# Attention into a GELU feed-forward on one core: V's path, the transposes' layout and the order of the start are changed

## The chip, the cores and the metric

One core of one Trainium2 chip runs the whole program. The metric is device time in microseconds; lower is better. Three runs of the kernel before took 374.42, 374.43 and 375.52 us, so its median is 374.43 us.

## What is computed

Attention is done inside chunks of 64 tokens, for 8 batches, 8 heads, 576 tokens (9 chunks) and head size 64. The heads' outputs stand side by side as 512 features of 4608 tokens, and these go through a feed-forward layer with exact GELU:

```python
q_c = q.reshape(B, H, nc, chunk, D)          # chunk = 64, D = 64
scores = scale * np.matmul(q_c, k_c.transpose(0, 1, 2, 4, 3))
attn = softmax(scores)
out = np.matmul(attn, v_c)
x = out.transpose(0, 2, 1, 3).reshape(B * S, H * D)   # 4608 x 512
h = x @ w_in                                           # 512 x 2048
y = gelu(h) @ w_out                                    # 2048 x 512
```

All inputs and the output are f32; the kernel computes its products in bf16.

## The kernel before, in words

The 4608 tokens are cut into 9 tiles of 512 tokens (8 chunks). A tile's attention has 4 groups `g`, each of 2 heads, and each group has three steps.

- **T** (`att_T`): TensorE transposes 4 pieces of Q and 4 of K into one PSUM tile `tp` (two such tiles exist). VectorE copies Q's half to `qT` and K's half, in two copies, into the block-diagonal `k_bd` (six exist; the off-diagonal blocks are zeroed once).
- **S** (`att_S`): 8 small matmuls give the scores `s_ps`, ScalarE applies Exp into `pT`.
- **B** (`att_B`): one matmul sums `pT`, 8 small ones multiply it with the block-diagonal `v_bd` into `av_ps`. VectorE transposes the sums (`t`), takes reciprocals (`r`), spreads them (`rc`) and multiplies (`x`).

`s_ps`, `sum_ps` and `av_ps` take turns in three PSUM buffers, so a B waits until an earlier user of its buffer is done.

The feed-forward of a tile has two phases of 16 slots: `mm1_slot` does 4 matmuls of 512 columns and a GELU on ScalarE, `mm2_slot` does 4 matmuls, and after each fourth slot VectorE copies `y_ps` to `y_sb` and SP stores it. The order of all engines is written out by hand: while tile t is in mm1 and tile t-1 in mm2, the steps T, S and B of tile t+1 are put between slots (`run_phase`, lines 232 to 267). Exp and GELU need different ScalarE tables, so each change from one to the other costs a table load.

Three queues bring data. SP issues the Q and K loads (line 98), f32, in pieces of 1 KB, and the stores. POOL issues the V loads (line 124) and the weight loads (lines 243 and 247), which change f32 to bf16 on the way; V's pieces are rows of 64 f32. POOL also casts Q and K of all tiles but the first (line 115). Its instructions run in order:

```python
new_tile(0)        # q, k on SP; 8 V loads on POOL; casts on VectorE and ScalarE
...                # 4 loads of w_in on POOL
new_tile(1)        # 16 V loads on POOL
...                # 2 loads of w_out on POOL
new_tile(2)        # 16 V loads on POOL
T, S_, Bs = att_units(0)
...
T, S_, Bs = att_units(1)     # tile 1's casts on POOL, behind all of these
```

A tile's 16 token columns of one transposed piece stand four tokens apart, and the kernel before carries this order through: `qT` keeps it, the copies into `k_bd` (line 157) and the multiplication into `x` (line 190) put it right as they write, so they write 2-byte elements 8 bytes apart.

Of the kernel before, what the change touches and what calls it, by code (L numbers as in the profile page):

```python
# [11 lines left out]
def kernel(  # L12
# [21 lines left out]
    CT = MT // CH  # L34
    G = H // 2
# [5 lines left out]
    FF = d_ff // P  # L41
# [15 lines left out]
    for i, t_ in enumerate(v_bds):
        nc.vector.memset(t_[0:CH, :, :, CH:P], 0.0)
        nc.vector.memset(t_[CH:P, :, :, 0:CH], 0.0)
    for t_ in k_bds:  # L60
        nc.vector.memset(t_[0:CH, :, CH:P], 0.0)
        nc.vector.memset(t_[CH:P, :, 0:CH], 0.0)
# [6 lines left out]
    ld = ctx.enter_context(tc.tile_pool(name="ld", bufs=3))  # L69
    work = ctx.enter_context(tc.tile_pool(name="work", bufs=3))  # L70
# [7 lines left out]
    def segments(t):  # L78

        segs = []  # L80
        c = t * CT
        while c < (t + 1) * CT:
            b, cs = divmod(c, NC)
            n = min(NC - cs, (t + 1) * CT - c)
            segs.append((c - t * CT, b, cs, n))
            c += n
        return segs

    def load_qk(t):
        st = {}  # L90
        raw = {nm: ld.tile([P, H, J, D], f32, tag=nm + "f", name=f"{nm}_f32", bufs=2) for nm in "qk"}
        for nm in "qk":
            st[nm] = ld.tile([P, G, J, 2, D], bf16, tag=nm, name=f"{nm}_nat", bufs=2)
        parts = [(h0, h0 + 2) for h0 in range(0, H, 2)] if t == 0 else [(0, H)]
        for h0, h1 in parts:
            for nm, src in (("q", q), ("k", k)):
                for i0, b, cs, n in segments(t):
                    nc.sync.dma_start(
                        raw[nm][PC * i0:PC * (i0 + n), h0:h1],
                        src[b, h0:h1, CH * cs:CH * (cs + n), :].rearrange(  # L100
                            "h (p j) d -> p h j d", j=J),
                    )
        def cast():
            for h0, h1 in parts:
                for nm in "qk":
                    o = st[nm][:, h0 // 2:h1 // 2].rearrange("p g j r d -> p g r j d")
                    i_ = raw[nm][:, h0:h1].rearrange("p (g r) j d -> p g r j d", r=2)
                    for g in range((h1 - h0) // 2):
                        if t == 0:
                            if nm == "q":  # L110
                                nc.vector.tensor_copy(o[:, g], i_[:, g])
                            else:
                                nc.scalar.copy(o[:, g], i_[:, g])
                        else:
                            nc.gpsimd.tensor_copy(o[:, g], i_[:, g])  # L115
        st["cast"] = cast
        return st

    def load_v(t):
        v_bd = v_bds[t % NV]  # L120
        for g in range(G):
            for r in range(2):
                for i0, b, cs, n in segments(t):
                    nc.gpsimd.dma_start(  # L124
                        v_bd[CH * r:CH * (r + 1), i0:i0 + n, g, CH * r:CH * (r + 1)],
                        v[b, 2 * g + r, CH * cs:CH * (cs + n), :].rearrange(
                            "(i key) d -> key i d", key=CH),
                    )
        return v_bd

    tiles = {}

    def new_tile(t):
        st = load_qk(t)
        st["v"] = load_v(t)
        tiles[t] = st
        if t == 0:
            st["cast"]()
# [34 lines left out]
    def att_B(t, g):  # L173
        st = tiles[t]
        pT = st["pT", g]
        sum_ps = ps_at.tile([P, CT * CH], f32, tag="at", name="sum_ps")
        nc.tensor.matmul(sum_ps[:], ones_bd[:], pT[:], start=True, stop=True)  # L177
        av_ps = ps_at.tile([P, CT, CH], f32, tag="at", name="av_ps")
        for i in range(CT):
            nc.tensor.matmul(av_ps[:, i, :], st["v"][:, i, g, :], pT[:, i, :],  # L180
                             start=True, stop=True)
        NB = MT // 32
        t1 = work.tile([P, NB, 32], f32, tag="t1", name="t1")
        nc.vector.transpose(t1[:], sum_ps[:].rearrange("p (n e) -> p n e", e=32))  # L184
# [47 lines left out]
    def run_phase(slot_fn, t, n, extra):  # L232
        for s in range(n):
            for u in extra.get(s, ()):
                u()
            slot_fn(t, s)

    with tc.manual_schedule():
        new_tile(0)
# [4 lines left out]
        new_tile(1)  # L244
# [53 lines left out]
```

## Time and profile before

| | |
|---|---|
| median of the runs | 374.43 us |
| the profiled execution, its own time | 375.98 us |
| its span, from first to last instruction | 374.2 us |
| TensorE busy | 305.2 us, 82% of the span |
| VectorE busy | 239.6 us, 64% |
| ScalarE busy | 140.2 us, 37% |
| POOL busy | 125.2 us, 33% (without its DMA issues' waits) |
| HBM read / written | 36.70 / 9.44 MB |

The shares are means over stages that differ: a start, a long stretch in which the tiles repeat, and an end. The stages are read apart below. All positions are microseconds from the start of the span.

### The profile page before, as it was taken

The page shows a single profiled execution, that of the slowest core. Times are in us where ns is not written, and L with a number is a line of the kernel's source. Part 1 is how long each engine was busy: PE and PEld are TensorE (multiplying, and loading weights), DVE is VectorE, ACT ScalarE, POOL GpSimd, SP SyncE. Part 2 cuts the span into 40 slices and gives each one's busy share as a digit, 9 for nine tenths or more (in the row PEclk, how much of TensorE's full clock was granted, in tenths as well). Part 3 has the DMA queues.
Part 4 walks back from the last instruction along what each step waited for, and adds up shares of the span by engine and source line. Part 5 has one row for each costly group of instructions (what it writes and reads, how often), then busy time and mean ns, then how long its engine had stood idle before and what let it go on. Part 6 is the DMA issues. An engine that isn't in the chain of part 4 may idle for free.

```text
span 374.2 us, 5238 instructions
## 1 busy us (share of the span) xinstructions
PE 305.2 (82%) x2052; PEld 154.5 (41%) x2052; DVE 239.6 (64%) x313; ACT 140.2 (37%) x208; POOL 125.2 (33%) x204
## 2 busy tenths in 40 slices
PE   0353500766899999999999999999999999999995
PEld 0241100332454555455445544544544455444442
DVE  7989100696775975887598589759867965920221
ACT  2130200189564066236505622551563165254000
POOL 7321855989700007703920780270130000000000
PEclk9999955598999999999999999999999999999999
DMA  9999899894700094848649483890800200010212
GB/s 209 256 247 243 56 174 98 145 127 29 46 2 29 30 228 66 102 119 161 66 50 218 71 85 108 198 84 30 257 26 28 87 0 30 30 56 0 86 56 84
DMA packets 67352, 37.57 MB, mean 100 GB/s; under 512 B 40192, under 2 KB 62720, under 8 KB 67328
## 3 DMA queue, kind: packets, MB, share of 16 engines
q1 hardware_dynamic: 24224, 28.32, 28.4%
q0 software_dynamic: 43104, 8.92, 26.9%
q8 instruction: 16, 0.26, 0.3%
q14 instruction: 8, 0.07, 0.1%
HBM read 36.70 MB, written 9.44 MB: 123 GB/s over the span
## 4 chain that ended last, share of the span: by engine, by line
PE 65%; DVE 14%; DMA 13%; POOL 4%; issue 2%; DVEq 0%; POOLq 0%
PE h_ps L212 30%; PE y_ps L224 28%; DMA w_in_sb<-in_moe_w_in_dram 7%; DVE x L190 4%; DMA w_out_sb<-in_moe_w_out_dram 4%; PE tp L148 4%; POOL v_bd L124 3%; DMA v_bd<-in_v_dram 3%; DVE rc L188 3%; DVE k_bd L157 3%; DVE t L184 3%; PE s_ps L167 1%; PE av_ps L180 1%; PE sum_ps L177 1%; DVE r L186 1%
## 5 line engine op out<-in xcount | busy, mean ns | idle before, releaser
L212 PE MATMUL h_ps<-x,w_in_sb 128*128 128x512 bf16 x576 | 138.1, 390 | 4.4 <-DVE x L190 4.3
L214 ACT ACTIVATE h<-h_ps 128x512 bf16<-128x512 f32 x144 | 85.5, 597 | 144.7 <-PE h_ps L212 144.5
L224 PE MATMUL y_ps<-w_out_sb,h 128*128 128x512 bf16 x576 | 132.5, 379 | 0.0
L124 POOL DMA_DIRECT2D v_bd<-in_v_dram x128 | 83.9, 713 | 29.4 <-DMA w_in_sb<-in_moe_w_in_dram 12.8
L157 DVE COPY k_bd<-tp 64x512 bf16<-64x512 bf16 x72 | 92.6, 1287 | 0.5
L212 PEld LDWEIGHTS <-w_in_sb 128*128 128x128 bf16 x576 | 55.7, 100 | 65.4 <-issue 9.3
L224 PEld LDWEIGHTS <-h 128*128 128x128 bf16 x576 | 53.5, 98 | 58.1
L228 DVE COPY y_sb<-y_ps 128x512 f32<-128x512 f32 x36 | 24.5, 695 | 60.4 <-PE y_ps L224 60.4
L115 POOL CAST q_nat<-q_f 128x512 bf16<-128x512 f32 x32 | 18.4, 637 | 106.8 <-PE h_ps L212 58.6
L190 DVE TENSOR_TENSOR x<-av_ps,rc 128x512 bf16<-128x512 f32 x36 | 46.5, 1292 | 4.1 <-DVE rc L188 0.5
L150 DVE COPY qT<-tp 128x512 bf16<-128x512 bf16 x36 | 15.2, 423 | 51.6 <-PE tp L148 51.4
L148 PE MATMUL tp<-ident,q_nat 128*128 128x128 bf16 x144 | 15.5, 236 | 39.7 <-POOL q_nat L115 22.6
L170 ACT ACTIVATE pT<-s_ps 128x512 bf16<-128x512 f32 x36 | 21.4, 597 | 34.9 <-PE s_ps L167 34.0
L148 PEld LDWEIGHTS <-q_nat 128*128 128x128 bf16 x144 | 11.7, 106 | 50.3 <-POOL q_nat L115 23.1
L184 DVE STREAM_TRANSPOSE t<-sum_ps 128x512 f32<-128x512 f32 x36 | 25.7, 715 | 8.8 <-PE sum_ps L177 8.8
L188 DVE STREAM_TRANSPOSE rc<-r 128x512 f32<-128x512 f32 x36 | 25.6, 711 | 1.3
L180 PEld LDWEIGHTS <-v_bd 128*128 128x128 bf16 x288 | 14.1, 101 | 23.4 <-issue 17.5
L180 PE MATMUL av_ps<-pT,v_bd 128*128 128x64 bf16 x288 | 15.4, 198 | 9.8 <-DVE x L190 5.8
L115 POOL CAST k_nat<-k_f 128x512 bf16<-128x512 f32 x32 | 18.4, 628 | 8.5 <-DMA k_f<-in_k_dram 7.8
L214 ACT ACT_TABLE_LOAD x12 | 15.4, 1283 | 10.6 <-PE h_ps L212 10.4
L167 PEld LDWEIGHTS <-k_bd 128*128 128x128 bf16 x288 | 13.9, 102 | 12.5 <-DVE k_bd L157 3.7
L177 PE MATMUL sum_ps<-pT,ones_bd 128*128 128x512 bf16 x36 | 14.8, 411 | 4.9 <-DVE x L190 4.8
(24 smaller groups left out, 88.5 us busy)
## 6 DMA issues: line engine op xcount, KB each, us to landing
out_dram<-y_sb SPq DMA_DIRECT2D x36, 256.0 KB, 2.0
w_in_sb<-in_moe_w_in_dram POOLq DMA_DIRECT2D x4, 512.0 KB, 23.0
w_out_sb<-in_moe_w_out_dram POOLq DMA_DIRECT2D x2, 1024.0 KB, 11.3
q_f<-in_q_dram SPq DMA_DIRECT2D x2, 896.0 KB, 9.1
k_f<-in_k_dram SPq DMA_DIRECT2D x2, 896.0 KB, 11.5
q_f<-in_q_dram SPq DMA_DIRECT2D x6, 256.0 KB, 6.8
k_f<-in_k_dram SPq DMA_DIRECT2D x6, 256.0 KB, 7.4
q_f<-in_q_dram SPq DMA_DIRECT2D x2, 768.0 KB, 11.6
```

The lines of the kernel that those rows point to most:

```text
L115: nc.gpsimd.tensor_copy(o[:, g], i_[:, g])
L124: nc.gpsimd.dma_start(v_bd[CH * r:CH * (r + 1), i0:i0 + n, g, CH * r:CH * (r + 1)], v[b, 2 * g + r, CH * cs:CH * (cs + n), :].rearrange("( ...
L148: nc.tensor.transpose(tp[:, w, j, :], st[nm][:, g, j].rearrange("p r d -> p (r d)"), ident[:])
L157: nc.vector.tensor_copy(k_bd[sl, :, sl].rearrange("p i (c j) -> p j i c", j=J), tp[sl, 1].rearrange("p j (i c) -> p j i c", i=CT))
L180: nc.tensor.matmul(av_ps[:, i, :], st["v"][:, i, g, :], pT[:, i, :], start=True, stop=True)
L184: nc.vector.transpose(t1[:], sum_ps[:].rearrange("p (n e) -> p n e", e=32))
L188: nc.vector.transpose(rc[:], r1[:].to_broadcast([P, NB, 32]))
L190: nc.vector.tensor_tensor(x[:, g, :].rearrange("p (i c j) -> p i j c", i=CT, j=J), av_ps[:].rearrange("p i (j c) -> p i j c", j=J), rc[:]. ...
L212: nc.tensor.matmul(h_ps[:], w_in_sb[:, ks, f * P:(f + 1) * P], st["x"][:, ks, :], start=(ks == 0), stop=(ks == KS - 1))
L214: nc.scalar.activation(st["h"][:, f, :], h_ps[:], Act.Gelu)
L224: nc.tensor.matmul(y_ps[:], st["h"][:, f, ms * P:(ms + 1) * P], w_out_sb[:, f, :], start=(f == 0), stop=(f == FF - 1))
L228: nc.vector.tensor_copy(y_sb[:], y_ps[:])
```

## The change

V is loaded by SP as f32 rows into a buffer `vf`, and cast from there into `v_bd`: tile 0's by ScalarE and POOL in two halves each, the other tiles' by POOL in two casts. The f32 buffers of Q and K are single now. The copies after the transposes and the multiplication into `x` all write in natural order; the copies read PSUM with the stride instead. Tile 0's casts go to VectorE, ScalarE and POOL, and one of its two `k_bd` copies to ScalarE. The zeroing of `v_bd` 1 and 2 and of `k_bd` 4 and 5 goes to POOL. In mm1 of tile 0, the steps of tile 1 stand in slots 10 to 15 and behind it (they stood in slots 4 to 15).

```diff
-        raw = {nm: ld.tile([P, H, J, D], f32, tag=nm + "f", name=f"{nm}_f32", bufs=2) for nm in "qk"}
+        raw = {nm: ld.tile([P, H, J, D], f32, tag=nm + "f", name=f"{nm}_f32", bufs=1) for nm in "qk"}
+        vf = ld.tile([P, G, CT, D], f32, tag="vf", name="v_f32", bufs=1)
...
-                    nc.gpsimd.dma_start(
-                        v_bd[CH * r:CH * (r + 1), i0:i0 + n, g, CH * r:CH * (r + 1)],
+                    nc.sync.dma_start(
+                        vf[CH * r:CH * (r + 1), g, i0:i0 + n, :],
                         v[b, 2 * g + r, CH * cs:CH * (cs + n), :].rearrange(
                             "(i key) d -> key i d", key=CH),
...
+        def cast_v(r, copy, gs=slice(0, G)):
+            sl = slice(CH * r, CH * (r + 1))
+            copy(v_bd[sl, :, gs, sl].rearrange("p i g d -> p g i d"), vf[sl, gs])
...
-        qT = work.tile([P, CT, J, PC], bf16, tag="qT", name="qT", bufs=6)
+        qT = work.tile([P, CT, CH], bf16, tag="qT", name="qT", bufs=6)
         nc.vector.tensor_copy(
-            qT[:].rearrange("p i j c -> p j i c"),
-            tp[:, 0].rearrange("p j (i c) -> p j i c", i=CT))
+            qT[:].rearrange("p i (c j) -> p i c j", j=J),
+            tp[:, 0].rearrange("p j (i c) -> p i c j", i=CT))
...
-            nc.vector.tensor_copy(
-                k_bd[sl, :, sl].rearrange("p i (c j) -> p j i c", j=J),
-                tp[sl, 1].rearrange("p j (i c) -> p j i c", i=CT))
+            copy = nc.scalar.copy if t == 0 and r == 1 else nc.vector.tensor_copy
+            copy(k_bd[sl, :, sl].rearrange("p i (c j) -> p i c j", j=J),
+                 tp[sl, 1].rearrange("p j (i c) -> p i c j", i=CT))
...
         nc.vector.tensor_tensor(
-            x[:, g, :].rearrange("p (i c j) -> p i j c", i=CT, j=J),
-            av_ps[:].rearrange("p i (j c) -> p i j c", j=J),
-            rc[:].rearrange("p n e -> p (n e)").rearrange("p (i j c) -> p i j c", i=CT, j=J),
-            op=mybir.AluOpType.mult)
+            st["x"][:, g, :], av_ps[:].rearrange("p i e -> p (i e)"),
+            rc[:].rearrange("p n e -> p (n e)"), op=mybir.AluOpType.mult)
...
+    def pool_casts(t):
+        for g in range(G):
+            for nm in "qk":
+                tiles[t]["cast"](nm, g, nc.gpsimd.tensor_copy)
+        for r in range(2):
+            tiles[t]["cast_v"](r, nc.gpsimd.tensor_copy)
...
-        run_phase(mm1_slot, 0, FF, {4: [T[0]], 5: [T[1]], 6: [T[2]], 7: [T[3]],
-                                    9: [S_[0]], 10: [S_[1]], 11: [S_[2], Bs[0]], 12: [S_[3]],
-                                    13: [Bs[1]], 14: [Bs[2]], 15: [Bs[3]]})
+        run_phase(mm1_slot, 0, FF, {10: [T[0]], 11: [T[1]], 12: [T[2], S_[0]], 13: [T[3], S_[1]],
+                                    14: [S_[2]], 15: [S_[3], Bs[0]]})
+        for u in Bs[1:]:
+            u()
```

POOL's queue at the start, before. `v_bd_67`, `_68` and `_69` belong to tiles 0, 1 and 2; `q_f_154` and `k_f_155` are tile 1's Q and K.

```order
L124 DMA v_bd_67<-in_v_dram 64x8x64 x7
L243 DMA w_in_sb<-in_moe_w_in_dram 128x4x512 x4
L124 DMA v_bd_68<-in_v_dram 64x64
...
L247 DMA w_out_sb<-in_moe_w_out_dram 128x8x512 x2
L124 DMA v_bd_69<-in_v_dram 64x2x64
...
L115 CAST q_nat<-q_f_154 128x2x4x64 x4
L115 CAST k_nat<-k_f_155 128x2x4x64 x4
```

And of the change, the same place (`q_f_254` and `k_f_255` are tile 1's):

```order
L120 CAST q_nat<-q_f_106 128x2x4x64 x2
L251 DMA w_in_sb<-in_moe_w_in_dram 128x4x512 x4
L124 CAST v_bd_67<-v_f_108 64x2x8x64 x2
...
L60 MEMSET v_bd_68 64x32x64
L61 MEMSET v_bd_68 64x32x64
L120 CAST q_nat<-q_f_254 128x2x4x64
L120 CAST k_nat<-k_f_255 128x2x4x64
...
L124 CAST v_bd_68<-v_f_256 64x4x8x64 x2
L270 DMA w_out_sb<-in_moe_w_out_dram 128x8x512 x2
```

Tile 1's casts stood behind 40 loads of V and all the weights; now they stand behind the 4 loads of w_in, tile 0's casts of V and some zeroing, and the loads of w_out stand behind them.

SP's queue at the start, of the change, with what each DMA waits for (`DMAHW0` to `DMAHW7` are the counters of DMAs on this queue; a later DMA on a counter waits for the landing of the one before it, here eight DMAs earlier).

```order
L105 DMA k_f_107<-in_k_dram 128x2x256
L113 DMA v_f_108<-in_v_dram 64x8x64 [waits DMAHW0_49]
L113 DMA v_f_108<-in_v_dram 64x8x64 [waits DMAHW1_49]
...
L105 DMA q_f_254<-in_q_dram 16x8x256 [waits DMAHW0_49,DVE_49,Pool_49]
L105 DMA q_f_254<-in_q_dram 112x8x256 [waits DMAHW1_49]
L105 DMA k_f_255<-in_k_dram 16x8x256 [waits DMAHW2_49,Activation_49]
L105 DMA k_f_255<-in_k_dram 112x8x256 [waits DMAHW3_49]
L113 DMA v_f_256<-in_v_dram 64x64 [waits DMAHW5_49,DMAHW6_49,DMAHW4_49,DMAHW7_49,Activation_49,Pool_49]
```

Tile 1's Q and K came directly behind tile 0's on this queue; now tile 0's V stands between them, they wait for tile 0's casts, and tile 1's V waits for tile 0's casts of V.

## Rows read from the trace of the kernel before

**Rows 1.** Busy time by stage: us, each engine's busy time (count), PEclk, DMA share, GB/s.

```profile
43.70:66.30 22.60, 0.03 (x1) 0.00 (x0) 0.00 (x0) 0.60 (x1) 14.20 (x23) 0.56 1.03 121
66.30:96.70 30.40, 21.18 (x151) 10.71 (x152) 23.33 (x28) 19.60 (x24) 29.40 (x50) 0.82 0.80 97
96.70:329.40 232.70, 226.84 (x1597) 116.10 (x1597) 176.78 (x224) 101.34 (x155) 63.31 (x103) 1.00 0.45 86
```

**Rows 2.** Waits, first 100 us: who waited for whom, total us, times, longest.

```profile
PE tp L148 <- POOL q_nat L115: 22.6, 1, 22.6
POOL v_bd L124 <- DMA w_in_sb<-in_moe_w_in_dram: 12.8, 4, 3.7
```

**Rows 3.** POOL in order of time: start, us, instruction, [idle before, releaser].

```profile
59.87 5.76 POOL L124 DMA_DIRECT2D v_bd<-in_v_dram  x9 [4.82 <-DMA w_out_sb<-in_moe_w_out_dram]
65.52 2.39 POOL L115 CAST q_nat<-q_f 128x512 bf16<-128x512 f32 x4
```

**Rows 4.** The chain that ended last: start, us, what.

```profile
95.38 1.29 DVE x L190
...
129.40 0.86 PE h_ps L212 x4
...
162.56 0.86 PE h_ps L212 x4
```

**Rows 5.** PE in steady state, in order of time.

```profile
120.30 0.44 PE L180 MATMUL av_ps<-pT,v_bd 128*128 128x64 bf16 x8 [0.83 <-DVE x L190]
```

**Rows 6.** DMA queues of the whole span: packets, MB, share of 16 engines.

```profile
q1 hardware_dynamic: 24224, 28.32, 28.4%
q0 software_dynamic: 43104, 8.92, 26.9%
```

**Rows 7.** Busy time by stage, as Rows 1, of two stretches full of loads.

```profile
48.00:58.00 10.00, 0.00 (x0) 0.00 (x0) 0.00 (x0) 0.00 (x0) 3.47 (x6) 0.50 1.19 190
...
2.30:38.90 36.60, 11.62 (x104) 7.80 (x105) 32.23 (x49) 6.03 (x9) 12.44 (x19) 1.00 1.27 247
```

**Rows 8.** DMA issues: count, KB each, us from issue to landing.

```profile
out_dram<-y_sb SPq DMA_DIRECT2D x36, 256.0 KB, 2.0
```

**Rows 9.** Groups by line and form: count, busy us, mean ns, idle before and releasers.

```profile
L157 DVE COPY k_bd<-tp 64x512 bf16<-64x512 bf16 x72 | 92.6, 1287 | 0.5
L190 DVE TENSOR_TENSOR x<-av_ps,rc 128x512 bf16<-128x512 f32 x36 | 46.5, 1292 | 4.1 <-DVE rc L188 0.5
L228 DVE COPY y_sb<-y_ps 128x512 f32<-128x512 f32 x36 | 24.5, 695 | 60.4 <-PE y_ps L224 60.4
L115 POOL CAST q_nat<-q_f 128x512 bf16<-128x512 f32 x32 | 18.4, 637 | 106.8 <-PE h_ps L212 58.6 <-DMA q_f<-in_q_dram 48.2
L150 DVE COPY qT<-tp 128x512 bf16<-128x512 bf16 x36 | 15.2, 423 | 51.6 <-PE tp L148 51.4
```

**Rows 10.** VectorE in order of time: the starts of two B groups.

```profile
90.57 0.72 DVE L184 STREAM_TRANSPOSE t<-sum_ps 128x512 f32<-128x512 f32 x1 [0.49 <-PE sum_ps L177]
...
93.52 0.72 DVE L184 STREAM_TRANSPOSE t<-sum_ps 128x512 f32<-128x512 f32 x1
```

**Rows 11.** ScalarE in order of time.

```profile
41.12 0.60 ACT L214 ACTIVATE h<-h_ps 128x512 bf16<-128x512 f32 x1 [1.11 <-PE h_ps L212]
42.82 0.60 ACT L214 ACTIVATE h<-h_ps 128x512 bf16<-128x512 f32 x1 [1.11 <-PE h_ps L212]
...
79.41 0.60 ACT L170 ACTIVATE pT<-s_ps 128x512 bf16<-128x512 f32 x1
80.02 1.28 ACT L214 ACT_TABLE_LOAD   x1
...
83.22 0.60 ACT L170 ACTIVATE pT<-s_ps 128x512 bf16<-128x512 f32 x1
...
98.44 0.60 ACT L214 ACTIVATE h<-h_ps 128x512 bf16<-128x512 f32 x1 [0.71 <-PE h_ps L212]
99.30 0.60 ACT L214 ACTIVATE h<-h_ps 128x512 bf16<-128x512 f32 x1 [0.27 <-PE h_ps L212]
```

More of the change, by code (lines that the diff above doesn't have):

```diff
@@ L56, with zero_v, zero_k @@
     k_bds = [consts.tile([P, CT, P], bf16, name=f"k_bd{i}") for i in range(NK)]
[L57 to L62, printed above, removed]
+    def zero_v(i):
+        eng = nc.vector if i == 0 else nc.gpsimd
+        eng.memset(v_bds[i][0:CH, :, :, CH:P], 0.0)
+        eng.memset(v_bds[i][CH:P, :, :, 0:CH], 0.0)
+    def zero_k(k_bd, eng):
+        eng.memset(k_bd[0:CH, :, CH:P], 0.0)
+        eng.memset(k_bd[CH:P, :, 0:CH], 0.0)
     w_in_sb = consts.tile([P, KS, d_ff], bf16, name="w_in_sb")
@@ L87, in segments, with load @@
         return segs
-    def load_qk(t):
+    def load(t):
         st = {}
-        raw = {nm: ld.tile([P, H, J, D], f32, tag=nm + "f", name=f"{nm}_f32", bufs=2) for nm in "qk"}
+        raw = {nm: ld.tile([P, H, J, D], f32, tag=nm + "f", name=f"{nm}_f32", bufs=1) for nm in "qk"}
+        vf = ld.tile([P, G, CT, D], f32, tag="vf", name="v_f32", bufs=1)
         for nm in "qk":
             st[nm] = ld.tile([P, G, J, 2, D], bf16, tag=nm, name=f"{nm}_nat", bufs=2)
+        v_bd = v_bds[t % NV]
+        st["v"] = v_bd
         parts = [(h0, h0 + 2) for h0 in range(0, H, 2)] if t == 0 else [(0, H)]
@@ L102, in load_qk @@
                     )
[L103 to L120, printed above, removed]
         for g in range(G):
@@ L128, in load_v, with cast @@
                     )
-        return v_bd
-    tiles = {}
[L133 to L138, printed above, removed]
+        def cast(nm, g, copy):
+            copy(st[nm][:, g].rearrange("p j r d -> p r j d"), raw[nm][:, 2 * g:2 * g + 2])
+        def cast_v(r, copy, gs=slice(0, G)):
+            sl = slice(CH * r, CH * (r + 1))
+            copy(v_bd[sl, :, gs, sl].rearrange("p i g d -> p g i d"), vf[sl, gs])
+        st["cast"], st["cast_v"] = cast, cast_v
+        tiles[t] = st
+    tiles = {}
     kcount = [0]
@@ L188, in att_B @@
         nc.vector.transpose(rc[:], r1[:].to_broadcast([P, NB, 32]))
-        x = st["x"]
         nc.vector.tensor_tensor(
-            x[:, g, :].rearrange("p (i c j) -> p i j c", i=CT, j=J),
-            av_ps[:].rearrange("p i (j c) -> p i j c", j=J),
-            rc[:].rearrange("p n e -> p (n e)").rearrange("p (i j c) -> p i j c", i=CT, j=J),
-            op=mybir.AluOpType.mult)
+            st["x"][:, g, :], av_ps[:].rearrange("p i e -> p (i e)"),
+            rc[:].rearrange("p n e -> p (n e)"), op=mybir.AluOpType.mult)
     def att_units(t):
-        if t:
-            tiles[t]["cast"]()
         tiles[t]["x"] = xpool.tile([P, G, MT], bf16, tag="x", name="x")
@@ L236, in run_phase @@
             slot_fn(t, s)
-    with tc.manual_schedule():
-        new_tile(0)
+    def pool_casts(t):
[4 more added lines that the diff above has]
+            tiles[t]["cast_v"](r, nc.gpsimd.tensor_copy)
+    with tc.manual_schedule():
+        zero_v(0)
+        load(0)
+        T, S_, Bs = att_units(0)
+        c0 = tiles[0]["cast"]
+        c0("q", 0, nc.vector.tensor_copy)
+        c0("k", 0, nc.scalar.copy)
+        for k_bd in k_bds[:G]:
+            zero_k(k_bd, nc.vector)
+        c0("q", 1, nc.vector.tensor_copy)
+        c0("k", 1, nc.scalar.copy)
+        T[0]()
+        c0("q", 2, nc.gpsimd.tensor_copy)
+        c0("k", 2, nc.scalar.copy)
+        T[1]()
+        S_[0]()
+        c0("q", 3, nc.gpsimd.tensor_copy)
         NWC = 4
@@ L243 @@
             nc.gpsimd.dma_start(w_in_sb[:, :, c * wc:(c + 1) * wc], w_in_v[:, :, c * wc:(c + 1) * wc])
-        new_tile(1)
+        c0("k", 3, nc.scalar.copy)
+        T[2]()
+        S_[1]()
+        T[3]()
+        S_[2]()
+        S_[3]()
+        for gs in (slice(0, 2), slice(2, 4)):
+            tiles[0]["cast_v"](0, nc.scalar.copy, gs)
+            tiles[0]["cast_v"](1, nc.gpsimd.tensor_copy, gs)
+        for k_bd in k_bds[G:]:
+            zero_k(k_bd, nc.gpsimd)
+        zero_v(1)
+        load(1)
+        for u in Bs:
+            u()
+        pool_casts(1)
         for c in range(2):
@@ L247 @@
             nc.gpsimd.dma_start(w_out_sb[:, fs], w_out_v[:, fs])
-        new_tile(2)
-        T, S_, Bs = att_units(0)
-        for u in T + S_ + Bs:
-            u()
-        T, S_, Bs = att_units(1)
-        run_phase(mm1_slot, 0, FF, {4: [T[0]], 5: [T[1]], 6: [T[2]], 7: [T[3]],
-                                    9: [S_[0]], 10: [S_[1]], 11: [S_[2], Bs[0]], 12: [S_[3]],
-                                    13: [Bs[1]], 14: [Bs[2]], 15: [Bs[3]]})
+        zero_v(2)
+        load(2)
+        T, S_, Bs = att_units(1)
+        run_phase(mm1_slot, 0, FF, {10: [T[0]], 11: [T[1]], 12: [T[2], S_[0]], 13: [T[3], S_[1]],
+                                    14: [S_[2]], 15: [S_[3], Bs[0]]})
+        for u in Bs[1:]:
+            u()
         for t in range(1, NT):
@@ L260 @@
                 T, S_, Bs = att_units(t + 1)
+                pool_casts(t + 1)
                 if t + 2 < NT:
-                    new_tile(t + 2)
+                    load(t + 2)
             run_phase(mm1_slot, t, FF, {1: [T[0]], 5: [T[1]], 9: [T[2]], 13: [T[3]]} if nxt else {})
```

## The prediction, written before the changed kernel ran

> **What bounds the kernel now.** I read the busy time by stage first. From 96.7 to 329.4 us TensorE is busy for 226.8 of 232.7 us: there it is the bound, and little can be won [rows 1]. Before that it is not: from 43.7 to 66.3 us it does nothing, and from 66.3 to 96.7 us it is busy for 21 of 30 us. The list of waits names the idle stretch: one wait of 22.6 us of tile 1's first transpose for a cast on POOL [rows 2]. POOL in order of time shows why: the cast starts at 65.52 us, directly behind V loads, the last nine of which were issued from 59.87 us on after a wait for w_out [rows 3]. POOL had also waited 12.8 us for w_in's loads to move on [rows 2]. So tile 1's casts, whose data had long been there, stood behind 40 V loads and all weights in one queue. In the chain of waits, x of tile 1 is complete at 95.38 + 1.29 = 96.67 us, and from there a period of the repeating part takes 162.56 - 129.40 = 33.16 us [rows 4]. In each period TensorE loses one piece that the profile shows: 0.83 us, where the second B's `av_ps` waits for the first B's x [rows 5].
>
> Three things set the answer, then: when tile 0's x is complete, how long mm1 of tile 0 with tile 1's attention takes, and the period.
>
> **V over SP's queue.** Tile 0's Q and K are 2.1 MB; at 247 GB/s, the rate of a stretch full of loads [rows 7], they take 8.5 us from 2.3 us on and end at 10.8. Then V, in 4096 pieces of 256 bytes. The trace has no such pieces on the hardware queue, so I bound them. By bytes at 247 GB/s a tile's V would take 4.2 us. By pieces at the hardware queue's mean, 0.284 x 374.2 x 16 / 24224 = 70 ns of one of 16 engines (its pieces are 1 KB and more), it takes 18 us. The software queue's mean is 37 ns, and most of its pieces are V's own 256-byte reads: 9.6 us [rows 6]. I take that nearest row.
>
> POOL issues w_in when it has cast two Q groups, at about 10.8 us, so w_in runs beside V. It is as large as w_out: 2.1 MB written, which at 190 GB/s [rows 7] take 11 us alone. With both queues full, the engines' share was 1.27 of one queue's [rows 7], so each moves at 0.64 of its speed. V of tile 0 is there at 10.8 + 9.6/0.64 = 25.8 us; one more us for DMAs that wait for the landing of the eighth before (a store lands in 2.0 us [rows 8]) makes 26.8. w_in is complete at 10.8 + 11/0.64 = 28. Tile 1's Q and K follow V: 8.5 us, a little of it shared, so 35.7.
>
> **Tile 0's x.** Q, K, the transposes and scores need nothing of V and are done by then. The second half of V is cast on ScalarE and POOL side by side: 1024 elements a partition at POOL's 637 ns for 512 [rows 9] are 1.3 us, so 28.1. Third `av_ps` and x follow at 29.4. A fourth group costs a pitch of VectorE's B chain, now 93.52 - 90.57 = 2.95 us [rows 10]. The new x writes contiguously: its nearest row is `y_sb`, 695 ns, against 1292 now [rows 9], so the pitch is 2.36 and x complete at 31.8 (before, at 38.7).
>
> **mm1 of tile 0 with tile 1's attention.** TensorE comes out of a stretch of small matmuls. The same slots before ran at half rate first: GELUs 1.70 us apart, against 0.86 later, although the profile's clock row says 1.00 there [rows 11]. With two slow slots, slots 0 to 9 take 2 x 1.7 + 8 x 0.86 = 10.3 us and end at 42.1. Tile 1's Q and K casts are 8 x 0.637 = 5.1 us on POOL behind 35.7, so 40.8: just in time, and each us later than 42.1 counts. Slots 10 and 11 with two transposes end at 44.7; the first scores follow. Then ScalarE sets the pace: Exp, load, GELU, load took 83.22 - 79.41 = 3.81 us a group before [rows 11] and do so here. The first Exp is done at 46.9, the fourth at 46.9 + 3 x 3.81 = 58.3. The second B's sums take the PSUM buffer that this fourth Exp frees, so three B groups still follow on VectorE: 58.6 + 3 x 2.36 + 0.2 = 65.9 us. Tile 1's V is there at 35.7 + 10.6 = 46.3, cast (2 x 2.55 us) by 51.4, ahead of the first B; w_out is issued behind it and needs 11 us, where mm2 starts only after 80: both are covered, with some 18 us to spare for w_out.
>
> So tile 1's x is complete at 65.9 in place of 96.67: **30.8 us earlier**. TensorE then comes out of a thin stretch (before, it did not: GELUs 0.86 us apart at 98.44 [rows 11]): three slow slots, +2.5 us.
>
> **The period.** TensorE stays the bound there. x of the first B comes 0.60 us earlier, so of the 0.83 us wait 0.58 goes, seven times: -4.1 us. The copies after the transposes write contiguously and read PSUM with a stride, of which the trace has no row. Bounds: 423 ns, what `qT` takes now, and 1287 ns, what the copies take that write with a stride [rows 9]; nothing excludes more, which is a rival below. I take 700 ns, `y_sb`'s one element a step. `qT` loses its quick form by this and the two `k_bd` copies gain, so VectorE's share a tile falls from 3.0 to 2.1 us a group, and all of it lies beside TensorE's work. Stores now share SP's queue with 20 loads a tile: 8.5 + 9.6 us of 33, and the loads stand ahead of the stores by half a period, so I cost that at nothing; if V ran at the upper bound, the first store would wait for some us in `y_sb`'s three buffers, still covered.
>
> The zeroing on POOL and tile 0's `k_bd` copies on ScalarE lie under V's loading. The end, 44.8 us from the last mm1 on, is untouched.
>
> **Sum.** -30.8 + 2.5 - 4.1 = -32.4 us. The profiled execution's own 375.98 us (span 374.2) become 343.6; the median of the runs is 1.55 lower, so **342 us**.
>
> **Rivals.**
>
> *The strided read costs what the strided write costs* (1.29 us a copy). A transposed group then holds VectorE for 3.9 us, the fourth scores of tile 1 come near 58.4 in place of being paced by ScalarE, and x of tile 1 some 3 us later; in the period VectorE would have 12 x 1.29 + 12.2 = 27.7 of 32.6 us, still covered. 345 us. For it: the copies' two-byte elements are 256 bytes apart in PSUM. Against it: what the row shows as slow is a write; no read with a stride is seen.
> The Trainium skill, Advanced Engine Details and Errata, section Memory Cachelines, speaks for this rival: it gives PSUM 8-byte lines and asks for every two consecutive elements to be contiguous. The same section lets SBUF run at full speed with two hits on a 16-byte line, and with that the trace disagrees for writes: 8 bytes apart, `k_bd`'s copy takes 1287 ns.
>
> *V's pieces cost what the hardware queue's pieces cost* (18 us a tile). V of tile 0 lands at 36, x is complete near 41, tile 1's V is cast only at 68.6, where the first B waits for it, and x of tile 1 is complete at 76.8: 353 us. For it: it is the queue that V moves to. Against it: those pieces are four times as large and more.
> The Trainium skill, DMA: Bandwidth & Descriptors, section Specifications, puts 512 bytes as the least for line rate. That leans to this rival; the 37 ns of the software queue are pieces below it as well.
>
> *VectorE becomes the bound, and the kernel slower.* A tile's copies are 12, and B chains and `y_sb` take 4 x 2.36 + 4 x 0.70 = 12.2 us; 12 c + 12.2 passes the period of 32.6 from c = 1.7 us on, and eats the whole gain from about 2.0. With twice the strided write, 2.57 us, the period is 43, and eight of them cost 84 us: about 426 us. Against it: no 512-element row of VectorE is above 1.3 us.
>
> *The wait on POOL stays in another form.* Tile 1's casts wait for loads that themselves wait for tile 0's casts (the Q and K buffers are single now). It takes back the gain only if these loads land near 69 us, 33 later than worked out: 374 us. I see nothing that would do it.
>
> **How the numbers follow.** The forecast has 0.62 (337 to 349 us by itself), the slow read 0.18, the slow V pieces 0.14, VectorE as the bound 0.03, POOL's wait 0.03. Faster means by over 0.3%, about what a measurement of this kernel can tell from no change: the first three, 0.94; the last I split in 0.02 the same and 0.01 slower, so 0.04 slower in all. The lower bound of V's pieces (4.2 us) would bring tile 0's x to about 23.4 and give 334 us; the upper one with the slow read 356. Cutting the outermost part of each, the range is 335 to 354.
>
> **What would show it.** Right: no idle stretch of TensorE over 5 us between 32 and 60 us; POOL's first cast of tile 1 near 36 us and not behind DMA issues; V of tile 0 landed at 24 to 29 us; Exp and GELU alternating in 3.8 us steps from 45 to 60 us; `x` and the copies near 0.7 us; a period of 32.6 us with 0.25 us left of the wait before `av_ps`. Wrong: copies above 1.2 us, tile 0's V after 33 us, a transpose of tile 1 that waits for POOL again, or a period that did not shrink.

## The result, and the profile after

The changed kernel took 338.14 us (median of four runs, 337.14 to 340.77) where the kernel before, beside it, took 374.98: a ratio of 0.902, 95% interval 0.896 to 0.908. Forecast were 342 us within 335 to 354. A repetition later gave 337.71 us and 0.896 (0.892 to 0.899). The profiled execution is the slowest of the four, 340.77 us with a span of 339.0; stages are compared by spans.

Page part 1 (busy time of each engine: us, share of the span, instructions) and the busy time by stage (columns as in [rows 1]):

```profile
PE 303.6 (90%) x2016; PEld 153.5 (45%) x2052; DVE 180.0 (53%) x299; ACT 144.9 (43%) x214; POOL 85.0 (25%) x104
```

```profile
0.00:30.00 30.00, 11.96 (x103) 7.11 (x105) 19.39 (x39) 11.72 (x16) 10.78 (x19) 1.00 0.98 213
30.00:62.50 32.50, 23.27 (x161) 11.15 (x164) 17.28 (x28) 22.21 (x28) 20.23 (x24) 0.88 0.97 182
62.50:80.40 17.90, 17.77 (x93) 8.76 (x94) 7.92 (x13) 8.96 (x15) 4.39 (x3) 0.84 1.03 188
80.40:294.00 213.60, 209.89 (x1478) 108.11 (x1504) 129.63 (x212) 92.50 (x139) 49.60 (x59) 1.00 0.48 112
```

From 80.4 to 294 us TensorE is busy for 209.9 of 213.6 us, as it was from 96.7 us on [rows 1]. It is at 90% of the span in place of 82%, for almost the same 304 us of work: the time came out of its idle stretches. The stretch of 22.6 us without work [rows 1] is gone. The first 62.5 us now end where tile 1's x is complete; that point was at 96.67 us.

TensorE's three largest waits of the first 100 us (total us, times, longest):

```profile
PE tp L139 <- DVE q_nat L120: 6.5, 2, 4.0
PE av_ps L171 <- POOL v_bd L124: 6.2, 1, 6.2
PE sum_ps L168 <- ACT pT L161: 4.6, 2, 3.2
```

The first is two waits for casts of tile 0's Q, whose loads are still on their way (4.0 us at the start of the span, 2.4 us from 5.5 on). The longest single one is 6.2 us, for tile 0's V. The wait of 22.6 us for a cast of tile 1's Q [rows 2] has no successor: the first transpose of tile 1 starts at 40.07 us without a wait. POOL in order of time shows the second half of V, tile 1's casts of Q and K, and those of its V:

```profile
25.05 1.04 POOL L124 CAST v_bd<-v_f 64x1024 bf16<-64x1024 f32 x1 [8.75 <-DMA v_f<-in_v_dram]
...
32.15 0.61 POOL L120 CAST q_nat<-q_f 128x512 bf16<-128x512 f32 x1
37.08 0.62 POOL L120 CAST k_nat<-k_f 128x512 bf16<-128x512 f32 x1 [4.32 <-DMA v_f<-in_v_dram]
...
40.43 0.62 POOL L120 CAST k_nat<-k_f 128x512 bf16<-128x512 f32 x1
43.51 3.85 POOL L124 CAST v_bd<-v_f 64x2048 bf16<-64x2048 f32 x2 [2.46 <-DMA v_f<-in_v_dram]
```

No cast waits behind issues of DMAs now: the first of tile 1 starts when POOL's zeroing ends, the second when a load lands (the profile names V's; in a repetition of the same kernel it names K's), and V's when its own loads land. TensorE in order of time, from tile 0's V to tile 1's x:

```profile
26.15 0.61 PE L171 MATMUL av_ps<-pT,v_bd 128*128 128x64 bf16 x8 [6.24 <-POOL v_bd L124]
...
30.00 10.24 PE L198 MATMUL h_ps<-x,w_in_sb 128*128 128x512 bf16 x37 [1.10 <-DVE x L180]
40.07 0.39 PE L139 MATMUL tp<-ident,q_nat 128*128 128x128 bf16 x4
...
49.27 0.38 PE L168 MATMUL sum_ps<-pT,ones_bd 128*128 128x512 bf16 x1
...
53.09 0.38 PE L168 MATMUL sum_ps<-pT,ones_bd 128*128 128x512 bf16 x1 [1.38 <-ACT pT L161]
...
56.91 0.58 PE L168 MATMUL sum_ps<-pT,ones_bd 128*128 128x512 bf16 x1 [3.21 <-ACT pT L161]
...
57.73 0.61 PE L168 MATMUL sum_ps<-pT,ones_bd 128*128 128x512 bf16 x1
...
62.58 0.59 PE L198 MATMUL h_ps<-x,w_in_sb 128*128 128x512 bf16 x1 [1.87 <-DVE x L180]
```

ScalarE in the same stretch (Exps of the first and fourth group; two GELUs of the next phase):

```profile
44.80 0.60 ACT L161 ACTIVATE pT<-s_ps 128x512 bf16<-128x512 f32 x1
...
56.26 0.60 ACT L161 ACTIVATE pT<-s_ps 128x512 bf16<-128x512 f32 x1
...
65.76 0.60 ACT L200 ACTIVATE h<-h_ps 128x512 bf16<-128x512 f32 x1 [1.96 <-PE h_ps L198]
67.47 0.60 ACT L200 ACTIVATE h<-h_ps 128x512 bf16<-128x512 f32 x1 [1.11 <-PE h_ps L198]
```

VectorE's groups by form, which answer to [rows 9], and the steady state, which answers to [rows 4] and [rows 5] (the chain, then TensorE in order of time):

```profile
L141 DVE COPY qT<-tp 128x512 bf16<-128x512 bf16 x36 | 24.9, 692 | 61.3 <-PE tp L139 61.2
L149 DVE COPY k_bd<-tp 64x512 bf16<-64x512 bf16 x68 | 46.5, 683 | 0.5
L180 DVE TENSOR_TENSOR x<-av_ps,rc 128x512 bf16<-128x512 f32 x36 | 24.9, 691 | 7.1 <-PE av_ps L171 3.4
L214 DVE COPY y_sb<-y_ps 128x512 f32<-128x512 f32 x36 | 24.7, 687 | 71.8 <-PE y_ps L210 71.8
```

```profile
130.87 0.86 PE h_ps L198 x4
...
163.40 0.86 PE h_ps L198 x4
```

```profile
88.40 0.39 PE L171 MATMUL av_ps<-pT,v_bd 128*128 128x64 bf16 x8 [0.23 <-DVE x L180]
```

The whole difference of the spans, 374.2 - 339.0 = 35.2 us, splits at two points that both traces have, tile 1's x and the first matmul of mm2 (into `y_ps`):

| | before | after | difference | forecast |
|---|---|---|---|---|
| tile 1's x complete | 96.67 | 61.83 + 0.69 = 62.52 | -34.15 | -30.8 |
| from there to the first `y_ps` | 15.16 | 17.85 | +2.69 | +2.5 |
| from there to the end | 262.37 | 258.63 | -3.74 | -4.1 |

### The profile page after: what moved, and what is told of

It reads as the page before. It is cut to its first block, busy times and chain, and to the rows that moved or that the text cites. A ratio compares the mean times of both kernels' runs of the same rounds, so it can differ in the third digit from the quotient of the medians.

```text
span 339.0 us, 5180 instructions
## 1 busy us (share of the span) xinstructions
PE 303.6 (90%) x2016; PEld 153.5 (45%) x2052; DVE 180.0 (53%) x299; ACT 144.9 (43%) x214; POOL 85.0 (25%) x104
## 3 DMA queue, kind: packets, MB, share of 16 engines
q1 hardware_dynamic: 63136, 37.76, 47.5%
## 4 chain that ended last, share of the span: by engine, by line
PE 78%; DVE 7%; DMA 5%; ACT 4%; SPq 2%; issue 2%; POOL 0%; DVEq 0%; ACTq 0%; POOLq 0%
PE h_ps L198 36%; PE y_ps L210 33%; PE tp L139 4%; DMA v_f<-in_v_dram 3%; DVE x L180 2%; DVE rc L179 2%; DVE t L175 2%; PE av_ps L171 2%; SPq L113 2%; DMA q_f<-in_q_dram 2%; PE sum_ps L168 2%; ACT L161 2%; PE s_ps L158 1%; ACT L200 1%; DVE r L177 1%
## 5 line engine op out<-in xcount | busy, mean ns | idle before, releaser
L198 PE MATMUL h_ps<-x,w_in_sb 128*128 128x512 bf16 x559 | 136.3, 390 | 5.3 <-DVE x L180 3.4
L210 PE MATMUL y_ps<-w_out_sb,h 128*128 128x512 bf16 x557 | 129.2, 379 | 1.0
L141 DVE COPY qT<-tp 128x512 bf16<-128x512 bf16 x36 | 24.9, 692 | 61.3 <-PE tp L139 61.2
L149 DVE COPY k_bd<-tp 64x512 bf16<-64x512 bf16 x68 | 46.5, 683 | 0.5
L120 POOL CAST q_nat<-q_f 128x512 bf16<-128x512 f32 x34 | 20.9, 615 | 93.6 <-DMA q_f<-in_q_dram 60.6
L124 POOL CAST v_bd<-v_f 64x2048 bf16<-64x2048 f32 (+1 forms) x18 | 32.4, 1798 | 35.9 <-DMA v_f<-in_v_dram 33.0
L180 DVE TENSOR_TENSOR x<-av_ps,rc 128x512 bf16<-128x512 f32 x36 | 24.9, 691 | 7.1 <-PE av_ps L171 3.4
L120 POOL CAST k_nat<-k_f 128x512 bf16<-128x512 f32 x32 | 19.7, 616 | 32.4 <-DMA k_f<-in_k_dram 24.2
L171 PEld LDWEIGHTS <-v_bd 128*128 128x128 bf16 x288 | 14.2, 103 | 23.9 <-issue 12.7
```

The source lines that it names most:

```text
L120: copy(st[nm][:, g].rearrange("p j r d -> p r j d"), raw[nm][:, 2 * g:2 * g + 2])
L124: copy(v_bd[sl, :, gs, sl].rearrange("p i g d -> p g i d"), vf[sl, gs])
L149: copy(k_bd[sl, :, sl].rearrange("p i (c j) -> p i c j", j=J), tp[sl, 1].rearrange("p j (i c) -> p i c j", i=CT))
L180: nc.vector.tensor_tensor(st["x"][:, g, :], av_ps[:].rearrange("p i e -> p (i e)"), rc[:].rearrange("p n e -> p (n e)"), op=mybir.AluOpTyp ...
L198: nc.tensor.matmul(h_ps[:], w_in_sb[:, ks, f * P:(f + 1) * P], st["x"][:, ks, :], start=(ks == 0), stop=(ks == KS - 1))
L210: nc.tensor.matmul(y_ps[:], st["h"][:, f, ms * P:(ms + 1) * P], w_out_sb[:, f, :], start=(f == 0), stop=(f == FF - 1))
```

## The experiments

Theory on record: tile 1's casts lost 22.6 us by their place on POOL, and the layout is worth 0.58 us a period. The rival that the traces alone don't exclude: V's move to the hardware queue is itself the gain. Ratios are to the kernel before, run beside each; their intervals are 95%.

**1. The layout alone.** In the kernel before:

```diff
-            qT[:].rearrange("p i j c -> p j i c"),
-            tp[:, 0].rearrange("p j (i c) -> p j i c", i=CT))
+            qT[:].rearrange("p i (c j) -> p i c j", j=J),
+            tp[:, 0].rearrange("p j (i c) -> p i c j", i=CT))
```

and the same for `k_bd` and `x`.

> The kernel before with the copies after the transposes and x in natural token order, and nothing else. My theory (the head's gain comes from what stands ahead of tile 1's casts on POOL; the layout is worth 0.58 us a period and little in the head): the 22.6 us wait of tile 1's first transpose stays, x writes take 0.69 us, the period falls by 0.58 us seven times (-4.1), tile 1's four B groups by 0.6 us once or twice (-1.5): about 369 us, ratio 0.985. Rival 1 (the layout also matters in the head, four B groups of two tiles at 0.6 us each): about 366. Rival 2 (the strided read costs what the strided write did): about 374.

Measured: 371.79 us, 0.987 (0.985 to 0.989). The wait of the first transpose did not stay, it grew:

```profile
PE tp L148 <- POOL q_nat L115: 30.7, 1, 30.7
```

Tile 0's x came 5.7 us earlier (the last mm1 matmuls of slot 0 start at 33.05 in place of 38.79), and all of that went into waiting for POOL: the first `y_ps` is at 112.13, in the kernel before at 111.83. From there to the end 4.6 us are won. The layout's worth in the head is nothing as long as POOL is late; my extra 1.5 us fell, the term for the period held.

**2. The change with the old layout.** The same edit in reverse, in the changed kernel.

> The changed kernel with the old layout of qT, k_bd and x (strided writes), all else as changed. My theory: the period goes back by 0.58 us seven times (+4.1), tile 0's four B groups and the two that follow tile 1's fourth Exp by 0.6 us each (+3.6): about 346 us, ratio 0.923. Rival (the copies matter too, because a transposed group holds VectorE for 3.0 us in place of 2.1 in the head): 350 or more.

Measured: 347.54 us, 0.924 (0.920 to 0.927). The slow writes are back, in groups by form:

```profile
L149 DVE COPY k_bd<-tp 64x512 bf16<-64x512 bf16 x68 | 87.5, 1287 | 0.5
L181 DVE TENSOR_TENSOR x<-av_ps,rc 128x512 bf16<-128x512 f32 x36 | 46.6, 1294 | 3.8
```

The spans differ by 7.1 us: 4.4 lie behind the first `y_ps` (263.1 us against 258.6), 2.7 ahead of it. The medians differ by 9.4 us, the ratios by 0.0215 or some 8 us, as forecast. With POOL out of the way the layout does count in the head.

**3. POOL's order alone.** In the kernel before, V still cast in flight on the software queue:

```diff
         st = load_qk(t)
+        if t == 1:
+            st["cast"]()
         st["v"] = load_v(t)
```

> The kernel before with tile 1's Q and K casts ahead of tile 1's V loads and w_out on POOL, V still cast in flight on the software queue. My theory (POOL's order is what cost): the 22.6 us wait goes, tile 1's transposes start near 44 us, x of tile 1 is complete near 72 in place of 96.7: about 351 us, ratio 0.936. Rival (V has to leave the software queue: tile 1's V, issued some 5 us later and behind w_in, now lands too late for the first B): 362 or more, with a wait of TensorE for v_bd's loads.

Measured: 357.70 us, 0.951 (0.945 to 0.956): between the two. TensorE's wait for tile 1's casts is gone and tile 1's x comes 25.3 us earlier (70.04 + 1.29), but the first `y_ps` is at 91.90, only 19.9 us earlier. POOL in order of time shows the same fault one tile on:

```profile
61.98 0.60 POOL L124 DMA_DIRECT2D v_bd<-in_v_dram  x1 [3.62 <-DMA w_out_sb<-in_moe_w_out_dram]
67.40 5.77 POOL L124 DMA_DIRECT2D v_bd<-in_v_dram  x9 [4.82 <-DMA w_out_sb<-in_moe_w_out_dram]
73.05 2.39 POOL L115 CAST q_nat<-q_f 128x512 bf16<-128x512 f32 x4
```

Tile 2's casts stand behind V loads, and these behind w_out's landing, until 73.05. TensorE waits 1.3 and 1.8 us for them, and the 16 matmuls of mm1 behind these waits take 4.78 us, where 16 later ones take 3.62; the granted clock is 0.50 from 76 to 78 us and 1.00 from 80 on.

**4. Both tiles' casts ahead.** `if t in (1, 2):` in the edit above.

> As the run with POOL's order alone, but tile 2's casts too stand ahead of tile 2's V loads. In that run x of tile 1 came 26 us earlier, but y started only 19.9 us earlier, since tile 2's casts still stood behind V loads that wait for w_out. If that is what held the rest back: y starts 3 to 4 us earlier than there, about 354 us. If instead the clock after the thin stretch or the loads themselves hold it: no change, 357 to 358.

Measured: 350.68 us, 0.930 (0.928 to 0.933). The first `y_ps` is at 86.47, 5.4 us earlier again, where 3 to 4 were forecast. The moved casts, without a byte on another queue, take 26.6 us; the change takes 37 to 39.

**5. V as f32 over POOL's software queue.** In the changed kernel:

```diff
-                    nc.sync.dma_start(
+                    nc.gpsimd.dma_start(
                         vf[CH * r:CH * (r + 1), g, i0:i0 + n, :],
```

> The changed kernel with V still f32 rows cast on chip, but loaded over POOL's software queue in place of SP's. Theory A (what counts is the order on POOL, not the queue): tile 0's V lands earlier (its loads no longer stand behind Q and K), x of tile 0 comes 2 to 4 us earlier; tile 1's V issues stand ahead of tile 1's casts on POOL, so these end 4 to 6 us later and TensorE waits some us for them: 336 to 345 us in all. Theory B (the hardware queue itself is the gain): 350 or more, with POOL's issues as the longest wait.

Measured: 352.45 us, 0.936 (0.933 to 0.939). Theory A's time was wrong, and tile 0's x came no earlier (30.4 us); TensorE waits for POOL again (the list of waits, first 100 us):

```profile
PE tp L139 <- POOL q_nat L120: 15.1, 4, 10.2
```

10.2 us of it fall on tile 2: its V issues wait for w_out as in run 3, and its casts stand behind them. Another 3.4 us fall on tile 1. Together they are 13.5 us, about as much as the spans differ (352.1 - 339.0 = 13.1). I had counted only tile 1's issues. So the number went to B, but the place of the loss is POOL's order once more. As V's loads are on the software queue here, the run by itself doesn't exclude the queue; the next one does.

**6. Order and layout, V's path untouched.** Runs 1 and 4 together, in the kernel before: nothing of V's f32 rows, its casts, the sharing, or the new slots.

> The kernel before with the casts of tiles 1 and 2 ahead of their V loads on POOL and with the natural layout, V still cast in flight on the software queue. Theory (V on the hardware queue is one way to clear POOL, not a gain of its own): the order gave a ratio of 0.930, the layout is worth 0.0215 between the changed kernel and the one with the old layout: 0.909, about 342 us. Rival (V's software queue costs more than its place on POOL): 0.925 or more, with waits of TensorE for v_bd's loads.

Measured: 338.90 us, 0.900 (0.897 to 0.903). The changed kernel, run beside it: 337.71 us.

> The changed kernel itself once more, to stand beside the next three on the same chip: a ratio of 0.902 within 0.006.

POOL in order of time:

```profile
24.99 2.29 POOL L115 CAST k_nat<-k_f 128x512 bf16<-128x512 f32 x4 [4.00 <-DMA k_f<-in_k_dram]
27.22 3.19 POOL L124 DMA_DIRECT2D v_bd<-in_v_dram  x5
...
54.56 2.31 POOL L115 CAST q_nat<-q_f 128x512 bf16<-128x512 f32 x4
```

The casts of tile 1 come before all V loads of tiles 1 and 2, those of tile 2 before tile 2's, and that, with the layout, brings all but 1.2 us of the change; the two intervals overlap. It is more than the 0.909 forecast: with both tiles' casts ahead the layout is worth 0.930 - 0.900 = 0.030, not the 0.0215 taken from run 2. The rival falls: V on the hardware queue clears POOL, and so does moving the casts. In the whole time V's new path, the sharing and the new slots together bring nothing measurable beyond. They do something in the head: tile 0's x is complete at 28.1 us in the changed kernel beside it and at 33.0 here, and the fourth Exp of tile 1 is done 4.75 us earlier (54.75 us against 59.50). But behind that Exp the changed kernel needs 5.7 us to tile 1's x and this one 3.0, and at the first `y_ps` 1.5 us are left (78.12 against 79.58).

**7. Without the sharing.** In the changed kernel all of tile 0's Q casts, both halves of `k_bd` and all zeroing on VectorE:

```diff
-        c0("q", 2, nc.gpsimd.tensor_copy)
+        c0("q", 2, nc.vector.tensor_copy)
...
-            copy = nc.scalar.copy if t == 0 and r == 1 else nc.vector.tensor_copy
+            copy = nc.vector.tensor_copy
```

> The changed kernel without the sharing of tile 0's work: its Q casts and k_bd copies on VectorE alone, its zeroing on VectorE. Theory (x of tile 0 waits for the second half of V, cast at 25.05 us, so all of it lies under V's loading): the same within 1 us, 338 to 339. Rival (the shared work is on the path to tile 0's scores and B groups): 341 or more.

Measured: 344.84 us, 0.915 (0.912 to 0.918). My theory fell: x of tile 0 is complete at 38.4 us in place of 29.9. But VectorE is not what was late. POOL, then ScalarE, in order of time:

```profile
1.27 0.89 POOL L251 DMA_DIRECT2D w_in_sb<-in_moe_w_in_dram  x1 [0.34 <-issue]
...
2.53 2.25 POOL L251 DMA_DIRECT2D w_in_sb<-in_moe_w_in_dram  x3
```

```profile
12.70 0.62 ACT L120 CAST k_nat<-k_f 128x512 bf16<-128x512 f32 x1 [7.83 <-DMA k_f<-in_k_dram]
```

POOL has no Q casts to do and issues w_in at 1.27 us, in the middle of Q's and K's loads; the second K group is cast at 12.70 us, behind a wait for its load, where the changed kernel casts it at 8.21.

**8. Only w_in held back.** Run 7 with one Q cast, the fourth, on POOL again, ahead of w_in's issues.

> The kernel without sharing, but with one Q cast, the fourth, on POOL again, ahead of w_in's issues. In the run without sharing POOL had nothing ahead of w_in, issued it from 1.3 us on, and tile 0's second K group was cast at 12.7 us in place of 8.2, after a wait for its load; x of tile 0 came 8.5 us later. If w_in beside Q and K is the cause: most of it comes back, ratio 0.902 to 0.907. Rival (VectorE's extra work on the path): it stays near 0.915.

Measured: 336.97 us, 0.894 (0.891 to 0.897), all of it back and no slower than the changed kernel (337.71, same chip). POOL in order of time:

```profile
9.17 0.61 POOL L120 CAST q_nat<-q_f 128x512 bf16<-128x512 f32 x1 [7.86 <-DMA q_f<-in_q_dram]
9.72 3.12 POOL L251 DMA_DIRECT2D w_in_sb<-in_moe_w_in_dram  x4
```

Tile 0's x is complete at 29.9 us again, 8.5 us earlier than in run 7: what counts most is that something on POOL waits for Q before w_in is issued. Casts, copies and zeroing shared over engines are worth nothing that shows in the whole time (the sharing of V's casts wasn't taken back). In the head they are worth 1.7 us up to tile 0's x (28.1 us in the changed kernel beside it), but there the 37 matmuls of mm1 behind it take 9.95 us, and here 8.15, at the full rate from their start, so that the first scores of tile 1 come at 41.2 and 41.1 us. The granted clock reads 1.00 in both stretches; why one of them starts at half rate isn't shown.

**9. The slots as before.** In the changed kernel tile 1's work back in slots 4 to 15.

> The changed kernel with tile 1's transposes, scores and B groups back in slots 4 to 15 of mm1 of tile 0, as before. Theory (Exp and GELU alternate at 3.8 us and set the pace, whichever slot they start in; the casts end at 41 us): the same time within 1.5 us, 337 to 340. Rival (a transpose in slot 4 waits for casts that end at 37.7 us and TensorE stands): 341 to 343.

Measured: 337.73 us, 0.896 (0.893 to 0.899): the same. A transpose does wait 2.5 us for POOL, and x of tile 1 comes at 63.7 us; but the mm1 that follows runs at full rate from its start (15.0 us to the first `y_ps` in place of 17.85; the granted clock is 1.00 from 60 us on, where the changed kernel has 0.50 until 67). Perhaps that is because TensorE had mm1 work between the B groups; it wasn't tried by itself.

**10. Exps together.**

```diff
-        run_phase(mm1_slot, 0, FF, {10: [T[0]], 11: [T[1]], 12: [T[2], S_[0]], 13: [T[3], S_[1]],
-                                    14: [S_[2]], 15: [S_[3], Bs[0]]})
+        run_phase(mm1_slot, 0, FF, {10: [T[0]], 11: [T[1]], 12: [T[2]], 13: [T[3]],
+                                    14: [S_[0], S_[1], S_[2], S_[3]], 15: [Bs[0]]})
```

> The changed kernel with tile 1's four score groups together in slot 14 of mm1 of tile 0, so that ScalarE alternates Exp and GELU once in place of four times. Theory (from 44.8 to 56.9 us the path is ScalarE's alternation at 3.82 us a group): fourth Exp done near 49, then four B groups at 2.36 us, x of tile 1 complete at 57 to 58 in place of 62.5, about 333.5 us. Rival (four B groups on VectorE, V's casts until 47.4 us, or the clock take it back): 336 to 338.

Measured: 336.29 us, 0.892 (0.889 to 0.894); against the changed kernel's two ratios, 0.902 and 0.896, the gain is small or nothing. ScalarE does what was meant:

```profile
45.14 1.28 ACT L161 ACT_TABLE_LOAD   x1
46.43 2.06 ACT L161 ACTIVATE pT<-s_ps 128x512 bf16<-128x512 f32 x4
48.51 1.28 ACT L200 ACT_TABLE_LOAD   x1
```

The fourth Exp is done at 48.5 us. But now four B groups follow it on VectorE, where in the changed kernel only two did, and x of tile 1 is complete 30.4 us after tile 0's in place of 32.6. Counted from tile 0's x, the fourth Exp came 6.5 us earlier (20.4 us in place of 26.9), and the B groups behind it took 4.3 of these back.

**11. Three edits to the head together.** Transposes from slot 9 with half of each `k_bd` copy on ScalarE, scores in slots 13 and 14, and

```diff
-        for c in range(NWC):
+        for c in (0, 1):
             nc.gpsimd.dma_start(w_in_sb[:, :, c * wc:(c + 1) * wc], w_in_v[:, :, c * wc:(c + 1) * wc])
```

with the other two issued behind tile 0's V casts.

> The changed kernel with three edits to its head: tile 1's transposes from slot 9 on, with one half of each k_bd copy on ScalarE as for tile 0; its scores in slots 13 and 14, so that ScalarE changes tables once; w_in's second half issued only behind tile 0's V casts. Theory: batching gives 0.011, the earlier slots some 2 us, tile 0's V comes 1 to 2 us earlier: a ratio of 0.88 to 0.886, about 331 us. Rival (w_in's second half lands too late for slot 8, or B groups wait for tile 1's V cast): no better than the batching alone, 0.891.

Measured: 334.11 us, 0.887 (0.883 to 0.891), against 337.71 us of the changed kernel on the same chip: 3.6 us less, with intervals that don't touch. It beats both kernels. Tile 0's x is complete near 26.0 us in place of 28.1 (run beside it), and tile 1's at 55.7 in place of 60.4. The ratio of 0.88 to 0.886 was not quite reached: ScalarE changed tables twice, not once. The fourth scores stand in slot 14, behind slot 13 and its GELU, and ScalarE takes that GELU first:

```profile
43.63 1.57 ACT L161 ACTIVATE pT<-s_ps 128x512 bf16<-128x512 f32 x3
...
46.51 0.60 ACT L200 ACTIVATE h<-h_ps 128x512 bf16<-128x512 f32 x1
...
48.42 0.60 ACT L161 ACTIVATE pT<-s_ps 128x512 bf16<-128x512 f32 x1
```

In run 10, with all four in one slot, the fourth scores waited for a PSUM buffer as they do here and still joined the batch. Which of the three edits carries how much wasn't tried.

## Why the prediction was right

- **The mechanism.** That tile 1's casts stood in POOL's order behind issues, and that this idle stretch was most of the gain, is shown by runs 3, 4 and 6: the moved casts take 26.6 us, casts and layout together 37.4 (376.29 - 338.90). The prediction put it on V's leaving POOL, which is what the change does; runs 4 and 6 show that the casts' place is enough. It didn't see one thing that run 3 found: with tile 1's casts alone moved ahead, the same wait comes again at tile 2.
- **V's loading.** Forecast 26.8 us; POOL casts the second half at 25.05, when its wait for V ends. With all other pieces at their old 70 ns, the hardware queue's row gives (0.475 x 339.0 - 0.284 x 374.2) x 16 / (63136 - 24224) = 22.5 ns of one engine for an added piece (V's rows are 36864 of the 38912), where 37 ns were taken:

```profile
q1 hardware_dynamic: 63136, 37.76, 47.5%
```

  By that price the landing would be near 21 us, by the prediction's own steps. ScalarE's half is indeed cast at 21.72; POOL's is later. What holds it, tile 1's Q and K issued from 14.2 us on or the waits between V's issues, was not settled. So 26.8 came near 25.05 partly by luck: the price of a piece was too high, and what held POOL's half stood in no term. The rival of 70 ns a piece fell. The Trainium skill, DMA: Bandwidth & Descriptors, section Specifications, gives 512 bytes as the least for line rate, which leaned to that rival. The trace doesn't bear out so high a price for 256-byte pieces; it doesn't show what larger ones of the same bytes would have cost.
- **Tile 0's x.** Forecast 31.8, measured 29.25 + 0.69 = 29.94: V's earlier landing.
- **"The second B's sums take the PSUM buffer that this fourth Exp frees, so three B groups still follow."** This is the term that failed, and most of the 3.3 us by which the head was better. The fourth Exp was forecast at 58.3 and done at 56.86; the steps of 3.81 us held (44.80 to 56.26 are three of 3.82). But the second sums wait only for the third Exp (53.09, behind 1.38 us) and the third sums for the fourth (56.91, behind 3.21 us): two groups follow, 5.66 us in place of 7.6. The three buffers are not taken in plain turns, and the trace before already showed it: its first `av_ps` of tile 1 waits for `t`, the reading of the same group's sums, so it took the buffer of its own sums. In plain turns it would have waited for the second Exp, which is done at 83.82 [rows 11].

```profile
81.77 0.47 PE L180 MATMUL av_ps<-pT,v_bd 128*128 128x64 bf16 x8 [1.34 <-DVE t L184]
```

  Run 8, with the same slots, shows a third pattern, in which only one group is left behind its fourth Exp (done at 54.67) and x is complete 3.3 us later; TensorE in order of time:

```profile
47.09 0.38 PE L168 MATMUL sum_ps<-pT,ones_bd 128*128 128x512 bf16 x1
...
50.10 0.38 PE L168 MATMUL sum_ps<-pT,ones_bd 128*128 128x512 bf16 x1 [0.57 <-DVE x L180]
...
51.29 0.38 PE L168 MATMUL sum_ps<-pT,ones_bd 128*128 128x512 bf16 x1
...
54.72 0.59 PE L168 MATMUL sum_ps<-pT,ones_bd 128*128 128x512 bf16 x1 [1.02 <-DVE rc L179]
...
58.02 0.58 PE L198 MATMUL h_ps<-x,w_in_sb 128*128 128x512 bf16 x1 [1.01 <-DVE x L180]
```

- **The clock.** Half-rate slots behind a thin stretch: forecast +2.5, measured +2.69. TensorE is busy for 0.6 us from 52 to 56 us; the granted clock is then 0.50 (1.2 GHz) from 56 to 67 us and 1.00 (2.4 GHz) from 69 on, and GELUs stand 1.71 us apart at 65.76 and 67.47. The two slow slots behind tile 0's x came as forecast too: its first GELUs stand 1.71 and 1.70 us apart (30.62, 32.33, 34.03), again at a granted clock of 1.00, and the first transpose of tile 1 follows x by 10.1 us, forecast 10.3.
- **The period.** 163.40 - 130.87 = 32.53, forecast 32.6; 0.23 us of the wait before `av_ps` is left, forecast 0.25.
- **The strided read.** Copies of 683 and 692 ns, as `y_sb` (687), which reads f32 without a stride: 700 was taken. The rival of 1.29 us fell. The Trainium skill, Advanced Engine Details and Errata, section Memory Cachelines, asks for pairs of consecutive elements in PSUM and spoke for it. The trace agrees in kind and not in that size: the copy into `qT` went from 423 ns [rows 9] to 692 when its read got the stride, while two-byte writes 8 bytes apart take 1287 ns (run 2).
- **The sharing, costed at nothing.** Right for the work in the whole time, as run 8 shows. The prediction did name the cast that holds w_in back, but gave it no price; it is 0.915 - 0.894 of the time before, or some 8 us, in runs 7 and 8.

## What to carry to other kernels

An engine that issues DMAs and also computes does both in one order: a cast whose data is there can wait tens of microseconds behind issues that wait for other landings. Look at that order before moving data to another queue, and follow the same fault into the next tile, where it may take back part of the gain. And a load that nobody needs yet is not free at the start: hold it until the loads on the path have landed.

## What the hardware showed that was not expected

- An added 256-byte piece on the hardware queue came to some 22.5 ns of one of 16 engines (an estimate, worked out above), below the 37 ns of the software queue's mean [rows 6].
- w_in issued 8.5 us earlier (1.27 us in place of 9.72, runs 7 and 8) made tile 0's x come 8.5 us later, 38.4 in place of 29.9: issued beside the loads on the path, it held them up by most of the 11 us that the prediction gave it for itself.
- Reading two-byte elements from PSUM 256 bytes apart took VectorE 683 to 692 ns for 512 elements, where a copy that reads and writes in longer runs took 423 [rows 9]; writing them 8 bytes apart took 1287.
- TensorE worked at half rate in stretches whose granted clock reads 1.00 (GELUs 1.70 us apart from 30.6 to 34.0 us in the changed kernel, 0.86 in run 8 at the same place): the clock row alone doesn't show it.
